# A planner that writes the instruction order of a fused attention and expert kernel: new prices, one shared port for VectorE and GpSimd, and a seeded first order

## The chip, the core and the metric

The kernel runs on one core of a Trainium2 chip. The core has five engines with one instruction queue each: TensorE (PE in the profile; PEld is its weight load), VectorE (DVE), ScalarE (ACT), GpSimd (POOL) and SyncE (SP), which here only issues transfers. Each engine takes its queue strictly in order and waits on semaphores where an instruction needs another engine's result. The metric is device time in microseconds (us), the median of several runs.

## The reference

Three parts follow each other. The intermediate values are float32, and every matrix product is made in float32 precision.

```python
q_n, k_n = (rmsnorm(q, g_q), rmsnorm(k, g_k))          # 4 batches, 12 heads, 448 tokens, 64 wide
scores = scale * np.matmul(q_n, k_n.transpose(0, 1, 3, 2))
attn = np.exp(scores - max) / sum
x = np.matmul(attn, v)                                  # laid out as 1792 tokens x 768
h = x @ w_in                                            # 768 x 2048
x = np.where(h > 0.0, h, np.exp(np.minimum(h, 0.0)) - 1.0) @ w_out
xn = x / rms * rms_g
out = (silu(xn @ w_gate) * (xn @ w_val)) @ w_out2       # 768 x 1536, twice, and back
```

## The kernel before

Attention is done in 24 **pairs** (two heads of one batch). A pair's steps are: load the tokens (`tk`), square them on ACT or POOL and sum the squares on DVE (`squares`), make the norm factors from the sums (`factors`, for several pairs at once, in `rr`), spread the factors along K (`spread`: for the first two pairs by small matmuls `bank<-ident,rr`, for all others by a round trip through DRAM, `scr<-rr` and `rb<-scr`), scale K (`rw<-rw,small,rb` on DVE), split Q and K into a high and a low part (`qh`, `ql`; pairs with odd numbers in the first batch use pieces of `gbig`), three matmuls per tile of scores (`s_group`), row maximum on DVE (`bank<-bank`, `nm`), exponential on ACT (`p`, `pj`, in odd pairs pieces of `tbig`), transposes on PE (`bank<-ident,p`), their copies out of PSUM (`pt`, `pe`), the product with V (`pv`), a multiplication with the reciprocal sums (`xf`) and a split into `xs`.

The expert layers are products `bank<-xs,w` and `bank<-gbig,w` with three matmuls each (high times high, high times low, low times high). They run in five stages: the first expert layers for batch 0, then for batch 1, the second ones for batches 0 and 1, and both again for batches 2 and 3, these last two stages with a scheme of seven products in place of eight (`quad`, with sums made ahead in `combos`). Weights are stored as 64-bit values. The first use of a chunk makes it into float32 (`w_convert`: two conversions on ACT or POOL, a mask and a merge on DVE: `wc`, `wt`) and keeps it in DRAM (`kept`); every use splits it into a high part (a copy on any engine, `w<-wc`) and a low part (a subtraction on DVE or POOL, `w<-wc,w`).

The order of all instructions on all engines is set by the class `Plan`. Each operation is entered with `plan.add`: the engines it may run on, a price in us for each, what it writes and reads. `schedule` then makes a first rank (the order of entry), plays the program through by `forward` (the engine that is free first takes the ready operation of the lowest rank; an operation that fits several engines goes to the one that would end it first), turns the result into new ranks by `backward`, and repeats this `PASSES` times. The play that ends first gives the order. The prices are written as functions: `c_v1` and `c_v2` for DVE, `c_a` for ACT, and numbers in place for POOL. Between dependent operations on different engines `LAT` is added. Two neighbours on DVE and POOL that both touch only SBUF stretch each other by the shares in `STRETCH`.

Of the kernel before, what the change touches and what calls it, by code (L numbers as in the profile page):

```python
# [35 lines left out]
class Plan:  # L36
# [4 lines left out]
    PASSES = 8  # L41
    LAT = 0.2
# [6 lines left out]
    STRETCH = {"v": 0.6, "g": 0.25}  # L49
# [36 lines left out]
    def add(self, alts, outs, ins, lag=0.0, after=None, soon=False, dma=False):  # L86
# [24 lines left out]
        shared = not any(getattr(ap.tensor, "_space", None) == PSUM for ap in list(outs) + list(ins) if ap is not None)  # L111
        self.ops.append((alts, preds, lag, soon, dma, shared))

    def schedule(self):
# [5 lines left out]
        best, rank = None, list(range(n))  # L120
# [10 lines left out]
    def backward(self, span, start, eng, price, lat):  # L131
# [8 lines left out]
        def avail(i):  # L140
            e, is_dma = eng[i], self.ops[i][4]
            r = 0.0 if self.succ[i] else lat[i]
            for s in self.succ[i]:
                if is_dma:
                    gap = lat[i] + 0.1
                elif eng[s] == e:
                    gap = 0.06 if e != "pe" else 0.0
                else:
                    gap = lat[i] + self.LAT
                r = max(r, left[s] + gap)  # L150
# [19 lines left out]
    def forward(self, rank):  # L170
# [14 lines left out]
        port = {"v": 0.0, "g": 0.0}  # L185
# [3 lines left out]
        def avail(i):  # L189
            for e in self.ops[i][0]:  # L190
                r = 0.0
                for j in self.ops[i][1]:
                    if self.ops[j][4]:
                        f = done[j] + 0.1
                    elif eng[j] == e:
                        f = done[j] - self.ops[j][2] + (0.06 if e != "pe" else 0.0)
                    else:
                        f = done[j] + self.LAT
# [7 lines left out]
        while left:  # L206
# [23 lines left out]
            i = heapq.heappop(now[e])[1]  # L230
            alts = self.ops[i][0]
            back[e] -= alts[e][0]
            if taken[i]:
                continue
# [11 lines left out]
            if e in self.STRETCH and self.ops[i][5]:  # L246

                o = "g" if e == "v" else "v"
                price += self.STRETCH[e] * max(0.0, min(port[o], t + price) - t)
                port[e] = t + price  # L250
# [11 lines left out]
            else:  # L262
                done[i] = free[e] + self.ops[i][2]
# [31 lines left out]
def kernel(ctx: ExitStack, tc: tile.TileContext, dims, tok, qk, vr, gq, gk, wst, rmsg, ident_in, out):  # L295
# [72 lines left out]
    def c_v1(n):  # L368
        return 0.15 + 0.00104 * n

    def c_v2(n):
        return 0.15 + 0.00052 * n

    def c_a(n):
        return 0.18 + 0.00083 * n

    def mm(o, l, r, start, stop, price=None):
        n = size(r)
        plan.add(
            {"pe": (price or max(0.108, n / 2400.0 + 0.017), lambda: T.matmul(o, l, r, start=start, stop=stop))},  # L380
            [o], [l, r] + ([] if start else [o]), lag=0.17,
        )

    def block(mms, price):
# [12 lines left out]
        plan.add({"pe": (price, go)}, list(outs.values()), list(ins.values()), lag=0.17)  # L397

    def transposes(pairs):
# [4 lines left out]
        plan.add({"pe": (0.02 + 0.11 * len(pairs), go)}, [o for o, _ in pairs], [i for _, i in pairs] + [ident], lag=0.17)  # L404

    def copy(dst, src, eng="vag"):
# [6 lines left out]
        if "a" in eng:  # L413
            alts["a"] = (c_a(n), lambda: A.activation(out=dst, in_=src, func=AF.Copy))
        if "g" in eng and not ps:
            alts["g"] = (
                0.2 + 0.00097 * n,
# [7 lines left out]
    def c_tt(a, b, n):  # L425
        return 0.2 + 0.0014 * n if two_sbuf(a, b) else c_v1(n)

    def tt(dst, a, b, op, eng="vg"):
# [4 lines left out]
        if "g" in eng and two_sbuf(a, b):  # L433
            alts["g"] = (0.25 + 0.0022 * n, lambda: G.tensor_tensor(out=dst, in0=a, in1=b, op=op))
# [18 lines left out]
    def act(dst, src, func, extra=0.0, accum=None, after=None, **kw):  # L453
        if accum is not None:
            kw["accum_out"] = accum
        plan.add(
            {"a": (c_a(size(src)) + extra, lambda: A.activation(out=dst, in_=src, func=func, **kw))},
# [3 lines left out]
    def vop(price, fn, outs, ins, after=None):  # L461
        plan.add({"v": (price, fn)}, outs, ins, after=after)

    def recip(dst, src):
        vop(0.15 + 0.00625 * size(dst), lambda: V.reciprocal(dst, src), [dst], [src])
# [164 lines left out]
    def w_convert(n):  # L630
# [13 lines left out]
                "a": (c_a(WN), lambda: A.activation(out=c, in_=Hf, func=AF.Copy, scale=2.0**-112)),  # L644
                "g": (
                    0.2 + 0.00097 * WN,
# [7 lines left out]
                "a": (0.3 + 0.001 * WN, lambda: A.activation(out=tl, in_=l8, func=AF.Copy, scale=1.0 / 32, bias=-15.5 / 32)),  # L654
                "g": (
                    0.3 + 0.00105 * WN,
# [780 lines left out]
```

## Time and profile before

| what | value |
|---|---|
| median of 3 runs | 1271.13 us (1270.31 to 1271.68) |
| the profiled execution, its own time | 1273.35 us |
| its span, first to last instruction | 1271.6 us |
| PE busy | 1231.3 us, 97% of the span, 6300 matmuls |
| POOL busy | 919.1 us, 72% |
| DVE busy | 835.1 us, 66% |
| ACT busy | 681.7 us, 54% |
| mean granted clock of TensorE | 0.993 |

PE is the engine that works nearly all the time; idle time of the other engines costs nothing as long as PE has work. Matmul ends are modelled, so a busy PE may hold short pauses. DVE and POOL are busy also while an instruction of theirs is held up after it was issued: two rows of one form with different durations show this.

### The profile page before, as it was taken

What the parts mean: (1) busy time and instruction counts of PE and PEld (TensorE: products, weight loads), DVE (VectorE), ACT (ScalarE), POOL (GpSimd) and SP (SyncE); (2) the same over time, 40 slices, a digit from 0 to 9 for tenths busy, and PEclk for the clock granted to TensorE, in tenths of its full rate; (3) what the DMA queues carried; (4) which work ended last, traced back from release to release, by engine and by line L of the source; (5) the groups of instructions that cost most, each with busy time, mean ns of one, the idle gap of its engine ahead of it and who ended that gap; (6) DMA issues with size and microseconds to landing.
All of it is one profiled execution on the core that took longest, in us unless ns stands there. A gap on an engine that the chain in (4) does not pass through costs nothing.

```text
span 1271.6 us, 17832 instructions
## 1 busy us (share of the span) xinstructions
PE 1231.3 (97%) x6300; PEld 1025.9 (81%) x6300; DVE 835.1 (66%) x1276; ACT 681.7 (54%) x1328; POOL 919.1 (72%) x688
## 2 busy tenths in 40 slices
PE   4998999999999999999999999999999999999998
PEld 2556867777777877898988888999999978999997
DVE  6886888879545588764554547626354899486582
ACT  5876767676655577554554543535334754342240
POOL 3587879997766697775653569948476999798680
PEclk9998999999999999999999999999999999999999
DMA  5677676775443444664444435212121112122112
GB/s 201 190 227 260 245 247 234 240 248 156 165 131 120 124 178 160 218 202 161 156 165 128 149 94 169 88 38 75 47 66 63 38 32 73 58 63 75 38 50 87
DMA packets 62206, 173.44 MB, mean 136 GB/s; under 512 B 10654, under 2 KB 19876, under 8 KB 62116
## 3 DMA queue, kind: packets, MB, share of 16 engines
q1 hardware_dynamic: 53476, 163.31, 39.3%
q10 hardware_dynamic: 8640, 8.99, 2.5%
q8 instruction: 49, 0.80, 0.2%
q14 instruction: 41, 0.34, 0.1%
HBM read 137.11 MB, written 35.17 MB: 135 GB/s over the span
## 4 chain that ended last, share of the span: by engine, by line
PE 79%; POOL 9%; DVE 4%; DMA 3%; issue 2%; ACT 1%; SPq 0%; ACTq 0%; POOLq 0%; DVEq 0%
PE bank L319 79%; POOL w L319 2%; POOL tbig L319 1%; POOL gbig L319 1%; POOL late L319 1%; POOL wr L319 1%; POOL xs L319 1%; DVE bank L319 1%; DMA rb<-scr 1%; DVE ybig L319 1%; POOL ql L319 1%; DMA tk<-tok 0%; DMA ybig<-tok 0%; DMA wc<-kept 0%; DMA wr<-wst 0%
## 5 line engine op out<-in xcount | busy, mean ns | idle before, releaser
L319 PE MATMUL bank<-xs,w 128*128 128x448 f32 x1872 | 423.0, 371 | 1.7 <-DVE tbig L319 0.9
L319 PE MATMUL bank<-gbig,w 128*128 128x448 f32 x1872 | 408.0, 372 | 2.8 <-POOL gbig L319 2.7
L319 PEld LDWEIGHTS bank<-gbig,w 128*128 128x128 f32 x1872 | 347.8, 189 | 43.0 <-issue 7.1
L319 PEld LDWEIGHTS bank<-xs,w 128*128 128x128 f32 x1872 | 344.6, 188 | 38.2 <-issue 6.7
L319 POOL TENSOR_TENSOR w<-wc,w 128x768 fp32r<-128x768 f32 (+1 forms) x126 | 241.8, 1921 | 81.1 <-ACT w L319 75.1
L319 DVE TENSOR_REDUCE bank<-bank 128x1 f32<-128x448 f32 x168 | 99.3, 624 | 76.2 <-PE bank L319 75.8
L319 ACT ACTIVATE w<-wc 128x768 fp32r<-128x768 f32 (+1 forms) x82 | 65.2, 795 | 91.7 <-PE bank L319 85.8
L319 DVE SCALAR_TENSOR_TENSOR wc<-wc,wt 128x768 int32<-128x768 int32 x68 | 92.2, 1356 | 26.9 <-ACT wc L319 16.5
L319 POOL TENSOR_TENSOR gbig<-tbig,gbig 128x448 fp32r<-128x448 f32 x75 | 99.8, 1333 | 8.7 <-ACT gbig L319 7.4
L319 ACT ACTIVATE p<-bank,nm,rr 128x448 f32<-128x448 f32 x126 | 90.2, 720 | 27.2 <-DVE nm L319 20.6
L319 POOL TENSOR_SCALAR w<-wc 128x768 fp32r<-128x768 f32 x65 | 60.9, 938 | 57.5 <-PE bank L319 51.6
L319 ACT ACTIVATE pt<-bank 128x384 f32<-128x384 f32 (+1 forms) x161 | 68.7, 448 | 50.6 <-PE bank L319 47.8
L319 DVE TENSOR_TENSOR tbig<-bank,tbig 128x448 f32<-128x448 f32 x80 | 48.5, 617 | 57.5 <-PE bank L319 55.4
L319 POOL TENSOR_TENSOR tbig<-tbig 128x448 f32<-128x448 f32 x45 | 59.5, 1324 | 28.3 <-DVE tbig L319 27.1
L319 DVE TENSOR_TENSOR ybig<-bank,ybig 128x448 f32<-128x448 f32 x72 | 44.4, 619 | 49.0 <-PE bank L319 48.8
L319 PE MATMUL bank<-ident,p 128*128 128x128 f32 x441 | 70.6, 277 | 5.4 <-ACT p L319 3.7
L319 PEld LDWEIGHTS bank<-ident,p 128*128 128x128 f32 x441 | 53.8, 141 | 23.0 <-ACT p L319 4.3
L319 PE MATMUL bank<-xs,late 128*128 128x448 f32 x288 | 69.5, 370 | 0.4 <-DVE xs L319 0.4
L319 DVE TENSOR_SCALAR wt<-wr 128x768 uint16<-128x768 uint16 x68 | 67.7, 995 | 1.5 <-DMA wr<-wst 1.2
L319 DVE SCALAR_TENSOR_TENSOR ybig<-bank,ybig 128x448 f32<-128x448 f32 x48 | 29.8, 622 | 55.1 <-PE bank L319 55.1
L319 PE MATMUL bank<-late,w 128*128 128x448 f32 x252 | 64.6, 368 | 0.0
L319 ACT ACTIVATE wt<-wr 128x768 uint16<-128x768 uint8 x42 | 45.7, 1089 | 28.6 <-DVE wc L319 20.7
(232 smaller groups left out, 2105.1 us busy)
## 6 DMA issues: line engine op xcount, KB each, us to landing
wr<-wst SPq DMA_DIRECT2D x68, 768.0 KB
wc<-kept SPq DMA_DIRECT2D x100, 384.0 KB
kept<-wc SPq DMA_DIRECT2D x68, 384.0 KB
rw<-qk SPq DMA_DIRECT2D x21, 512.0 KB
tk<-tok SPq DMA_DIRECT2D x20, 480.0 KB
rv<-vr SPq DMA_DIRECT2D x24, 256.0 KB
out_t<-ybig SPq DMA_DIRECT2D x24, 224.0 KB
rb<-scr ACTq DMA_DIRECT2D x36, 128.0 KB
```

The costliest lines, as they stand in the source:

```text
L319: return lambda *a, **k: f(*[real(x) for x in a], **{n: real(x) for n, x in k.items()})
```

## The change

All of it is in the planner and in the prices. No operation of the kernel is added or removed; which engine takes an operation, and in which place, may change. The change

- replaces `LAT` (0.2 for every hand-over between engines) by `HOP` (0.04 to 0.12, by receiving engine) and a `TAIL` that is added to the end of an operation but does not keep its engine;
- lets DVE and POOL share one `port`: every POOL operation takes it, and every DVE operation without PSUM operand unless it is marked `port=False` (reductions, reciprocals). While it is taken the other's operation waits and then is shortened by `BEHIND`. `STRETCH` goes;
- lets DVE take another ready operation, one that doesn't use the port, when the port is taken;
- prices an operation by the time from its issue to the next (`c_v1`, `c_v2`, `c_a`, new `c_gt` and `c_gs` for POOL), so nearly all prices fall;
- starts from the order of entry with seeded noise of up to 40 places, and makes 36 passes in place of 8.

```diff
-    PASSES = 8
-    LAT = 0.2
+    PASSES = 36
+    SEED = 20
+    HOP = {"pe": 0.12, "v": 0.04, "a": 0.04, "g": 0.09, "sp": 0.04}
+    TAIL = {"pe": 0.0, "v": 0.085, "a": 0.11, "g": 0.04, "sp": 0.0}
+    BEHIND = {"v": 0.15, "g": 0.05}
+    SLACK = 0.1
-    STRETCH = {"v": 0.6, "g": 0.25}
...
-        best, rank = None, list(range(n))
+        noise = random.Random(self.SEED)
+        best, rank = None, [i + 40 * noise.random() for i in range(n)]
...
+            if e == "v" and self.ops[i][5] and port > t + 0.1:
+                x = min((x for x in now["v"] if not taken[x[1]] and not self.ops[x[1]][5] and t + self.ops[x[1]][0]["v"][0] <= port + self.SLACK), default=None)
+                if x is not None:
+                    now["v"].remove(x)
+                    heapq.heapify(now["v"])
+                    heapq.heappush(now["v"], (rank[i], i))
+                    i = x[1]
...
-            if e in self.STRETCH and self.ops[i][5]:
-
-                o = "g" if e == "v" else "v"
-                price += self.STRETCH[e] * max(0.0, min(port[o], t + price) - t)
-                port[e] = t + price
+            if e == "g" or e == "v" and self.ops[i][5]:
+                if port > t:
+                    price = port - t + max(0.03, price - self.BEHIND[e])
+                port = t + price + self.TAIL[e]
...
-        return 0.15 + 0.00104 * n
+        return 0.064 + 0.00105 * n
...
-    def c_a(n):
-        return 0.18 + 0.00083 * n
+    def c_a(n, ps=False):
+        return (0.06 if ps else 0.1) + 0.00083 * n
+
+    def c_gt(n):
+        return 0.14 + 0.00216 * n
+
+    def c_gs(n):
+        return 0.155 + 0.00084 * n
...
-        return 0.2 + 0.0014 * n if two_sbuf(a, b) else c_v1(n)
+        return c_v1(n)
```

How many instructions each engine issues by the two orders: POOL 688 before and 607 now, ACT (its transfers included) 1279 and 1362, DVE 1276 and 1274, SP 388 and 388. What moved most: 36 copies of 128x768, 18 of 128x448 and 5 squarings of 128x960 from POOL to ACT, 16 additions or subtractions of 128x448 and 4 of 128x512 from POOL to DVE, 18 small copies out of PSUM from DVE to ACT.

Three places show what that does. The first is on POOL, where the first expert layer begins and pair 6 is prepared: `ql<-rw,qh` makes the low part of pair 6's K, `w` and `wc` are weights, `gbig<-tbig` are pieces of the hidden layer. Before:

```order
L319 TENSOR_TENSOR xs_75<-xf_124,xs_74 128x448
L319 TENSOR_SCALAR w_96<-wc_93 128x768
L319 TENSOR_SCALAR wc_92<-wr 128x768
L319 TENSOR_TENSOR w_96<-wc_93,w_96 128x768
L319 TENSOR_SCALAR w_97<-wc_94 128x768
L319 TENSOR_SCALAR wc_93<-wr 128x768
L319 TENSOR_TENSOR ql<-rw_101,qh 128x512
L319 TENSOR_SCALAR wt_95<-wr 128x768
L319 TENSOR_TENSOR gbig<-tbig,gbig 128x448
```

and now:

```order
L331 TENSOR_SCALAR wt_95<-wr 128x768
L331 TENSOR_SCALAR w_96<-wc_93 128x768
L331 TENSOR_TENSOR w_96<-wc_93,w_96 128x768
L331 TENSOR_TENSOR gbig<-tbig,gbig 128x448
L331 TENSOR_SCALAR gbig<-tbig 128x448
L331 TENSOR_SCALAR qh<-rw_101 128x512
L331 TENSOR_TENSOR gbig<-tbig,gbig 128x448
L331 TENSOR_TENSOR ql<-rw_101,qh 128x512
L331 TENSOR_TENSOR gbig<-tbig,gbig 128x448 x2
```

The weight work that stood between pair 6's high part and its low part is gone from there; one subtraction of 128x448 stands between them, and three `gbig` instructions are ahead of `ql`.

The second place is PE in the first pairs. `ident,rr` with 64x128 is the spread of the factors of pair 1, `qh` is pair 0, `gbig` is pair 1, `ident,p` are the transposes of pair 0. Before:

```order
L319 MATMUL bank7_132<-ident_61,rr0_112 64x128 x8
L319 MATMUL bank6_131<-ident_61,pj0_107 128x128 x3
L319 MATMUL bank6_131<-ident_61,pj0_107 64x128
L319 MATMUL bank1_126<-qh_103 128x448
L319 MATMUL bank2_127<-qh_103 128x448
...
L319 MATMUL bank4_129<-ident_61,p0_105 128x128 x3
L319 MATMUL bank6_131<-ident_61,p0_105 128x128 x3
L319 MATMUL bank3_128<-gbig_88 128x448 x3
L319 MATMUL bank5_130<-ident_61,rs0_119 7x128
```

and now (the spread of pair 1 stands above, right behind that of pair 0 and ahead of all matmuls of scores):

```order
L331 MATMUL bank6_131<-ident_61,pj0_107 128x128 x3
L331 MATMUL bank6_131<-ident_61,pj0_107 64x128
L331 MATMUL bank1_126<-qh_103 128x448
L331 MATMUL bank2_127<-qh_103 128x448
...
L331 MATMUL bank3_128<-gbig_88 128x448 x3
L331 MATMUL bank6_131<-ident_61,p0_105 128x128 x3
L331 MATMUL bank4_129<-ident_61,p0_105 128x128 x3
L331 MATMUL bank0_125<-gbig_88 128x448
```

The spread of pair 1 left its place between the scores, and three matmuls of pair 1 now stand ahead of pair 0's transposes.

The third place is ACT's queue where the factors of pairs 6 to 11 go to DRAM (`scr<-rr`; `tk` is a squaring of the tokens of a later pair). Before:

```order
L319 ACTIVATE ybig<-bank_131 128x384
L319 ACTIVATE tk_100<-tk_100 128x960
L319 ACTIVATE w_99<-wc_92 128x768
L319 DMA scr_148<-rr_113 128x8
L319 DMA scr_152<-rr_113 128x8
```

and now:

```order
L331 ACTIVATE wt_95<-wr 128x768
L331 ACTIVATE w_99<-wc_92 128x768
L331 ACTIVATE tk_100<-tk_100 128x960
L331 DMA scr_148<-rr_113 128x8
L331 ACTIVATE wt_95<-wr 128x768
L331 ACTIVATE xs_74<-xf_124 128x448
L331 DMA scr_152<-rr_113 128x8
```

In both a squaring that needs a transfer stands just ahead of the first `scr<-rr`. Counted from the start, 127 instructions of ACT are ahead of it before and 148 now, and squarings of batch 2's tokens are two before and three now.

## Rows read from the trace of the kernel before

**Rows 1.** The page's first part: busy time, share of the span, instructions.
```profile
PE 1231.3 (97%) x6300; PEld 1025.9 (81%) x6300; DVE 835.1 (66%) x1276; ACT 681.7 (54%) x1328; POOL 919.1 (72%) x688
```
**Rows 2.** Stretches: length, busy PE, PEld, DVE, ACT, POOL (instructions), PE's clock, DMA.
```profile
0.00:20.00 20.00, 4.92 (x25) 3.42 (x27) 11.96 (x34) 8.56 (x9) 5.08 (x9) 1.00 0.68 248
20.00:100.00 80.00, 72.60 (x422) 39.73 (x420) 67.15 (x159) 62.66 (x161) 51.86 (x47) 0.98 0.62 199
100.00:140.00 40.00, 35.40 (x160) 28.69 (x158) 27.09 (x33) 24.64 (x44) 30.90 (x22) 0.91 0.79 264
170.00:180.00 10.00, 7.80 (x33) 5.90 (x33) 7.75 (x11) 6.87 (x15) 9.84 (x8) 0.83 0.70 241
260.00:320.00 60.00, 56.66 (x292) 43.72 (x291) 52.36 (x85) 39.90 (x79) 50.99 (x37) 1.00 0.62 196
320.00:1000.00 680.00, 679.42 (x3503) 580.10 (x3502) 381.34 (x586) 351.99 (x679) 460.71 (x351) 1.00 0.39 126
1000.00:1090.00 90.00, 86.98 (x410) 76.72 (x409) 88.71 (x93) 50.28 (x86) 89.49 (x60) 0.98 0.16 49
1090.00:1272.00 182.00, 178.03 (x867) 162.34 (x865) 103.99 (x142) 54.51 (x86) 123.77 (x89) 1.00 0.19 61
```
**Rows 3.** Timeline at 11 us, DVE and POOL: start, duration, instruction.
```profile
11.79 1.14 DVE L319 SCALAR_TENSOR_TENSOR sn<-sn,rr 128x15 f32<-128x15 f32 x1
...
11.63 1.27 POOL L319 TENSOR_TENSOR gbig<-wr,gbig 128x512 fp32r<-128x512 f32 x1 [2.53 <-ACT gbig L319]
```
**Rows 4.** Timeline of PE, 20 to 31 us; in brackets idle time before, and releaser.
```profile
22.65 1.97 PE L319 MATMUL bank<-ident,rr 128*64 128x128 f32 x16
...
28.18 0.33 PE L319 MATMUL bank<-ident,p 128*128 128x128 f32 x1 [0.84 <-ACT p L319]
29.95 0.76 PE L319 MATMUL bank<-ident,p 128*128 128x128 f32 x4 [1.44 <-ACT p L319]
```
**Rows 5.** Timeline of PE, 112 to 122 us.
```profile
118.75 0.47 PE L319 MATMUL bank<-ql,qh 128*128 128x448 f32 x1 [2.89 <-POOL ql L319]
...
121.41 1.11 PE L319 MATMUL bank<-gbig,w 128*128 128x448 f32 x2 [0.70 <-POOL gbig L319]
```
**Rows 6.** Timeline of POOL, the same stretch.
```profile
114.36 1.55 POOL L319 TENSOR_SCALAR w<-wc 128x768 fp32r<-128x768 f32 x1
115.87 0.89 POOL L319 TENSOR_SCALAR wc<-wr 128x768 f32<-128x768 f32 x1
116.72 1.98 POOL L319 TENSOR_TENSOR ql<-rw,qh 128x512 fp32r<-128x512 f32 x1
```
**Rows 7.** Two stretches of 10 us, columns as in rows 2.
```profile
120.00:130.00 10.00, 9.30 (x36) 6.61 (x35) 9.12 (x13) 7.45 (x16) 9.92 (x7) 0.70 0.76 235
...
1020.00:1030.00 10.00, 7.84 (x29) 5.59 (x28) 10.00 (x7) 5.70 (x12) 10.00 (x7) 0.85 0.00 1
```
**Rows 8.** Timeline, 1013 to 1025 us: POOL, DVE, PE.
```profile
1013.89 1.54 POOL L319 TENSOR_TENSOR late<-ybig,late 128x448 fp32r<-128x448 f32 x1
1015.38 1.54 POOL L319 TENSOR_TENSOR tbig<-tbig,rsb 128x448 f32<-128x448 f32 x1
...
1014.33 1.57 DVE L319 TENSOR_TENSOR ybig<-ybig 128x448 f32<-128x448 f32 x1
...
1024.41 0.68 PE L319 MATMUL bank<-late,late 128*128 128x448 f32 x2 [0.94 <-POOL late L319]
```
**Rows 9.** Groups by form: count, busy us, mean ns, idle before and releasers.
```profile
L319 POOL TENSOR_SCALAR w<-wc 128x768 fp32r<-128x768 f32 x65 | 60.9, 938 | 57.5 <-PE bank L319 51.6 <-DVE wc L319 2.7 <-DVE nm L319 1.5
...
L319 ACT ACTIVATE w<-wc 128x768 fp32r<-128x768 f32 x70 | 59.0, 843 | 81.9 <-PE bank L319 76.0 <-issue 3.1 <-DMA wc<-kept 2.1
```
**Rows 10.** Who waited for whom: total us, times, longest.
```profile
PEld bank L319 <- ACT p L319: 6.5, 7, 1.6
```
**Rows 11.** The chain that ended last, 91 to 101 us: start, length, what.
```profile
91.50 5.91 DMA tk<-tok
...
97.50 3.72 DMA scr<-rr
```

More of the change, by code (lines that the diff above doesn't have):

```diff
@@ L84, in region, with add @@
         return ap.name, halves, m
-    def add(self, alts, outs, ins, lag=0.0, after=None, soon=False, dma=False):
+    def add(self, alts, outs, ins, lag=0.0, after=None, soon=False, dma=False, port=True):
         i = len(self.ops)
@@ L110, in add @@
                 self.hist[name] = keep
-        shared = not any(getattr(ap.tensor, "_space", None) == PSUM for ap in list(outs) + list(ins) if ap is not None)
+        shared = port and not any(getattr(ap.tensor, "_space", None) == PSUM for ap in list(outs) + list(ins) if ap is not None)
         self.ops.append((alts, preds, lag, soon, dma, shared))
@@ L184, in forward @@
         taken = [False] * n
-        port = {"v": 0.0, "g": 0.0}
+        port = 0.0
         dma_free = 0.0
@@ L194, in avail @@
                         f = done[j] + 0.1
-                    elif eng[j] == e:
-                        f = done[j] - self.ops[j][2] + (0.06 if e != "pe" else 0.0)
+                    elif e == "pe" and eng[j] == "pe":
+                        f = done[j] - self.ops[j][2]
                     else:
-                        f = done[j] + self.LAT
+                        f = done[j] + self.HOP[e]
                     r = max(r, f)
@@ L262, in forward @@
             else:
-                done[i] = free[e] + self.ops[i][2]
+                done[i] = free[e] + self.ops[i][2] + self.TAIL[e]
             dur[i], lat[i] = price, done[i] - t - price
@@ L379, in mm @@
         plan.add(
-            {"pe": (price or max(0.108, n / 2400.0 + 0.017), lambda: T.matmul(o, l, r, start=start, stop=stop))},
-            [o], [l, r] + ([] if start else [o]), lag=0.17,
+            {"pe": (price or max(0.108, n / 2400.0 + 0.0165), lambda: T.matmul(o, l, r, start=start, stop=stop))},
+            [o], [l, r] + ([] if start else [o]), lag=0.16,
         )
@@ L396, in block @@
             ins[id(l)], ins[id(r)] = l, r
-        plan.add({"pe": (price, go)}, list(outs.values()), list(ins.values()), lag=0.17)
+        plan.add({"pe": (price, go)}, list(outs.values()), list(ins.values()), lag=0.16)
     def transposes(pairs):
@@ L402, in go @@
                 T.transpose(o, i, ident)
-        plan.add({"pe": (0.02 + 0.11 * len(pairs), go)}, [o for o, _ in pairs], [i for _, i in pairs] + [ident], lag=0.17)
+        plan.add({"pe": (0.02 + 0.11 * len(pairs), go)}, [o for o, _ in pairs], [i for _, i in pairs] + [ident], lag=0.16)
     def copy(dst, src, eng="vag"):
@@ L455, in act, with vop @@
             kw["accum_out"] = accum
+            extra += 0.09
+        if any(hasattr(kw.get(k), "tensor") for k in ("scale", "bias")):
+            extra += 0.09
         plan.add(
-            {"a": (c_a(size(src)) + extra, lambda: A.activation(out=dst, in_=src, func=func, **kw))},
+            {"a": (c_a(size(src), in_psum(src)) + extra, lambda: A.activation(out=dst, in_=src, func=func, **kw))},
             [dst, accum], [src] + [x for x in kw.values() if hasattr(x, "tensor") and x is not accum], after=after,
         )
-    def vop(price, fn, outs, ins, after=None):
-        plan.add({"v": (price, fn)}, outs, ins, after=after)
+    def vop(price, fn, outs, ins, after=None, port=False):
+        plan.add({"v": (price, fn)}, outs, ins, after=after, port=port)
     def recip(dst, src):
-        vop(0.15 + 0.00625 * size(dst), lambda: V.reciprocal(dst, src), [dst], [src])
+        vop(0.1 + 0.00625 * size(dst), lambda: V.reciprocal(dst, src), [dst], [src])
     def dma(dst, src, nbytes, after=None, soon=False, by="sp"):
@@ L661, in w_convert @@
         )
-        vop(0.15 + 0.00104 * WN, lambda: V.tensor_scalar(out=th, in0=h16, scalar1=0x8000, scalar2=None, op0=ALU.bitwise_and), [th], [h16])
+        vop(c_v2(WN), lambda: V.tensor_scalar(out=th, in0=h16, scalar1=0x8000, scalar2=None, op0=ALU.bitwise_and), [th], [h16], port=True)
         stt(ci, ci, 3, ti, ALU.logical_shift_left, ALU.bitwise_or)
```

38 lines of the change are left out of this document (20 added, 18 removed).

## Prediction

> **What bounds the kernel now.** I read the page's busy times first, then a table by stretches, then the timeline of PE where that table shows it idle. PE is busy for 1231.3 of 1271.6 us [rows 1], so 40.3 us is all the idle time that a better order could win, and no other engine is near that share. Where it lies is in [rows 2], length less PE's busy time: 15.1 us before 20 us (first loads and first norm), 7.4 between 20 and 100 (attention of batch 0 alone), 4.6 from 100 to 140 (the expert layer starts), 2.2 at 170 to 180, 3.3 from 260 to 320, 0.6 in the 680 us to 1000, 3.0 from 1000 to 1090, and 3.6 at the end (the last result on its way out). What lies between these stretches is the missing 0.5. The first loads and the end don't depend on how the rest is ordered, save for a little at 10 to 20 us. So some 21 us is open. To it comes TensorE's clock. Behind idle time it was granted 1.2 in place of 2.4 GHz for short times: 0.70 on the mean of 120 to 130 us, behind the waits that ended at 118.75, and 0.85 at 1020 to 1030 [rows 5, 7]. By the clock column of [rows 2] this loses 0.02 x 80 + 0.09 x 40 + 0.17 x 10 + 0.02 x 90 = 8.7 us. Together 30 us, 2.4% of the span, is about the most that can be won, and two thirds of it lies in the first 320 us.
>
> Page and row differ on that ceiling. The Trainium skill ("Perfetto Trace Analysis", Identifying the Most-Contended Engine) calls matmul busy time a bad measure and weight-load busy time a good one: PEld has 81% of the span against 89% (162.34 of 182) in the last stretch, which would leave room for some 120 us, and a time near 1150 (1025.9 / 0.89). I don't follow it: from 20 to 100 us PEld is at 50% while PE is at 91% [rows 2], because transposes and products with V load weights for less time than they stream; the mix explains the difference. Short pauses inside busy time may exist all the same (a rival below).
>
> **The old plan's error.** A tiny DVE instruction of 15 elements took 1.14 us while POOL ran a subtraction from 11.63 to 12.90 [rows 3]: DVE was held until POOL was done. The old plan charges such a pair a share of the overlap; the new one charges the whole. Where the pieces of DVE and POOL alternate, one addition on each takes 1.49 us (POOL's starts at 1013.89 and 1015.38, the DVE addition between them 1.57) [rows 8]. So the new description of the port is the one the trace shows, and the new order should meet fewer surprises on those two engines. POOL also has less to do: 36 copies at 0.938 us are 33.8 us [rows 9], moved to ACT at 0.843.
>
> **The sum, stretch by stretch** (idle time plus clock is what can be won; the other bound in brackets):
>
> *0 to 20 us.* The spread of pair 1 costs PE 1.97 us at 22.65 [rows 4]. Now it stands ahead of the scores, while PE waits for K of pair 0 anyway. Against it, that order also makes the scores wait for what DVE does for pair 1, and a reduction stands ahead of the scaling of K. I take -1 (from -2 to +1).
>
> *20 to 100 us.* 7.4 idle and 1.6 clock. The two largest waits I see there, 0.84 and 1.44 us, are transposes that wait for the exponential [rows 4]; three matmuls of pair 1 now stand ahead of them and fill about 0.6 us. But ACT gets fuller: 21 more instructions ahead of the first `scr<-rr`, at 0.84 at most 17.6 us, on top of 62.66 busy of 80 [rows 2, 9]. That would be 80 of 80, by this high price. I take -2.5 (from -6 to +5; +5 if ACT becomes the bound and a third of the 17.3 us that it idled there stays on top of its 80, since it must go on waiting for DVE and PE at some points).
>
> *100 to 140 us.* 4.6 idle and 3.6 clock. PE waited 2.89 us for pair 6's `ql`, which stood on POOL behind a weight copy of 1.55 and a conversion of 0.89 and itself took 1.98 [rows 5, 6]. In the new order one `gbig` subtraction stands between `qh` and `ql`. 2.4 us of foreign work go, one piece of some 1.1 to 1.5 comes; and by the order of PE, 84 in place of 69 matmuls of the expert layer precede pair 6's scores, 15 more matmuls of cover. The wait should vanish, and with it the low clock behind it. K itself may still come late (its factors go out behind a squaring that waits for its tokens, as before: the load was under way for 5.91 us [rows 11]). I take -5 (from -8 to 0).
>
> *170 to 180 us.* 2.2 idle, 1.7 clock; the same kind of wait for POOL, which is busy 9.84 of 10 [rows 2]. I take -2.5 (from -3.9 to 0).
>
> *260 to 320 us.* 3.3 idle, clock full, POOL and DVE both at 51 to 52 of 60. POOL's copies moved to ACT, which has 20 us free there [rows 2]. I take -2 (from -3.3 to 0).
>
> *1000 to 1090 us.* 3.0 idle, 1.8 clock. DVE and POOL are at 98 and 99% [rows 2], so the port is the limit and PE waits for what it makes (0.94 us for `late` at 1024.41 [rows 8]). Here the two orders have nearly the same work: between the first and the last addition that reads `ybig`, 24 POOL and 20 DVE additions of 128x448 before, 25 and 18 now. The 12 of the 16 moved additions that lie in the last two stages are splits of `gbig`, elsewhere. So only the order inside can help. I take -1.5 (from -4.8 to +2).
>
> *New waits.* A new order meets its own surprises, where the old one had none: 140 to 170, 180 to 260, 320 to 1000 us. The prices of transfers are not changed by the diff, so their errors stay. I take +1.5 (0 to +6).
>
> Sum: -1 - 2.5 - 5 - 2.5 - 2 - 1.5 + 1.5 = **-13 us**: a span of 1258.6, a time of 1260.3 for an execution like the profiled one (its 1273.35 is 1.75 above its span). The median shown is 2.2 below that execution, so I forecast **1258 us**.
>
> **Rivals.**
>
> *More comes back* (1247). PE's busy time may hide pauses of a few tenths, since ends are modelled, and the first 320 us could give all of their idle and clock. For it: from 20 to 100 us the engines all have gaps at the same time, which points at the order and not at work. All 21 + 8.7 less the 6 of port-bound loss would be -24. Against it: ACT's load.
>
> *The waits only move* (1268). PE is at 97%, and each wait that goes may show the next one: K of pair 6 came by a chain of transfers (5.91 for tokens, 3.72 for the factors [rows 11]) whose prices stay as wrong as they were. Then 100 to 140 and 1000 to 1090 us gain nothing, the rest half: about -4, and with new waits -3.
>
> *Slower: ACT as the new bottleneck of attention* (1280). The change moves copies onto the engine that also does the exponentials and empties PSUM for PE. In the trace a wait of PE's weight load for `p` is 6.5 / 7 = 0.93 us [rows 10]; a copy of 0.843 us put in front of an exponential is of that size. One more such wait in each of 24 pairs is 22.3 us, and 22.3 - 13 = +9. It decides from 14 pairs on (14 x 0.93 = 13). Against it: after 320 us ACT is busy 352 of 680 us, and PE has expert matmuls beside the pairs to fill a late one; only 6 pairs stand alone.
>
> *The plan's description does no good* (within 0.2%, which is about what a measurement of this kernel can tell from no change). The list rule with 8 passes may already have found waits that only transfers cause. Against it: the rows at 118.75 and 1024.41 name POOL.
>
> **Chances and range.** Forecast, a gain of 6 to 19 us: 0.48. More: 0.14. Waits only move: 0.16, a quarter of it within 0.2% (2.5 us). No good: 0.06. Slower: 0.16, of which 0.02 is within 0.2%. That makes faster 0.74, same 0.12, slower 0.14. The range holds 8 in 10: below it a little of "more" (all 30 us would be 1241), above it the worse half of "slower". 1244 to 1273; the forecast's own range is 1252 to 1265.
>
> **What would show it.** Right: PE idle from 100 to 140 us under 2 us and its clock there above 0.97; `ql` of pair 6 on POOL within 2 us of its `qh`, with no wait of PE for it; tiny DVE instructions with means near their least; POOL's busy time down by some 50 to 90 us, ACT's up by some 45 to 70 (83 instructions more, at most at the 0.84 of a copy); the loss from 1000 to 1090 us nearly as before. Wrong: waits of PE or PEld for ACT `p` and `pt` above 15 us in total; ACT above 90% from 20 to 100 us with that stretch no shorter; a wait for `rb<-scr` ahead of pair 6 that holds PE for more than 3 us; new idle time of PE between 320 and 1000 us above 3 us.

## The result, and the profile after

The changed kernel takes 1261.41 us (median of 4 runs, 1256.58 to 1262.78) against 1270.72 us of the kernel before beside it: a ratio of 0.9919 (95% interval 0.9891 to 0.9947), 9.3 us faster. The forecast was 1258 us, in a range of 1244 to 1273. The profiled execution took 1256.58 us, the fastest of the four, with a span of 1254.8 us, 16.8 below that of before; so its rows show more than the typical gain (see the first experiment).

The page's first part, which answers to [rows 1]:

```profile
PE 1222.4 (97%) x6300; PEld 1026.5 (82%) x6300; DVE 832.4 (66%) x1274; ACT 729.1 (58%) x1411; POOL 837.2 (67%) x607
```

The stretches of [rows 2], with the same columns, in the changed kernel:

```profile
0.00:20.00 20.00, 2.63 (x20) 2.18 (x22) 11.78 (x35) 9.19 (x10) 4.09 (x8) 1.00 0.71 254
20.00:100.00 80.00, 77.61 (x429) 43.43 (x430) 62.07 (x152) 71.54 (x181) 40.60 (x37) 1.00 0.62 201
100.00:140.00 40.00, 35.89 (x169) 30.85 (x168) 26.30 (x36) 28.04 (x49) 22.91 (x18) 0.91 0.78 256
...
170.00:180.00 10.00, 9.80 (x61) 8.12 (x60) 8.90 (x16) 8.24 (x19) 9.45 (x7) 1.00 0.70 232
...
260.00:320.00 60.00, 58.79 (x316) 46.92 (x316) 47.96 (x81) 43.77 (x92) 48.21 (x37) 1.00 0.59 185
320.00:1000.00 680.00, 680.00 (x3511) 584.83 (x3510) 387.66 (x586) 386.19 (x728) 423.06 (x305) 1.00 0.39 124
1000.00:1090.00 90.00, 88.03 (x425) 78.93 (x425) 79.61 (x87) 45.02 (x74) 85.94 (x57) 1.00 0.20 60
```

POOL lost 82 us and ACT took 47, as forecast. PE's idle time went from 40.3 to 32.4 us, 7.9 less. The head got worse (idle 15.1 to 17.4), 100 to 140 us stayed (4.6 to 4.1, clock 0.91 both times), 20 to 100 got better by 5.0.

The clock column seems to give 5.1 us more (0.007 x 1271.6 = 8.9 us lost before, 0.003 x 1254.8 = 3.8 now), but it can't be used for the start. The trace's clock records begin at 26.95 us before and at 38.8 us now, and the column counts the time ahead of the first record as full clock. The pace of the matmuls tells otherwise. Timeline of PE, changed kernel, the same form at 35 and at 57 us:

```profile
35.41 1.49 PE L331 MATMUL bank<-gbig 64*128 64x448 f32 x6
...
57.08 0.86 PE L331 MATMUL bank<-gbig 64*128 64x448 f32 x6
```

Until 38 us PE ran at the pace of the lower level (1.2 GHz), and 1.49 in place of 0.86 us means that some 42% of such time is lost. With the time ahead of the first record counted, PE was busy at the lower level for 27.8 us before and 25.9 us now, which is an estimated loss of 11.7 and 10.9 us. So the clock gave about 1 us on the whole: some 2 us more lost before 100 us (15.3 and 20.6 us busy at the lower level), some 3 us less behind. PE's busy time fell by 8.9 us; 8.1 of them the clock doesn't explain, and what they were (pauses hidden by the modelled ends, perhaps) stays open.

Idle time alone misleads here, so here is the same table in long stretches, to be read by the matmuls that each holds (the number behind PE's busy time; 320 to 1000 us stands in [rows 2] and above). Before:

```profile
0.00:100.00 100.00, 77.52 (x443) 43.15 (x445) 79.10 (x192) 71.22 (x170) 56.93 (x56) 0.98 0.64 208
100.00:320.00 220.00, 209.39 (x1085) 163.60 (x1082) 181.91 (x268) 153.71 (x308) 188.18 (x135) 0.98 0.71 233
...
1000.00:1320.00 320.00, 265.00 (x1275) 239.06 (x1273) 192.70 (x234) 104.78 (x172) 213.26 (x148) 0.99 0.15 49
```

and after:

```profile
0.00:100.00 100.00, 80.24 (x447) 45.60 (x448) 73.85 (x187) 80.73 (x191) 44.69 (x44) 1.00 0.64 212
100.00:320.00 220.00, 212.92 (x1130) 168.53 (x1129) 181.27 (x275) 169.38 (x345) 170.22 (x124) 0.98 0.72 239
...
1000.00:1320.00 320.00, 249.21 (x1217) 227.56 (x1216) 189.63 (x229) 92.78 (x148) 199.23 (x136) 1.00 0.15 49
```

By 100 us only 4 matmuls more were done (0.8 us): what the idle time gained there, the clock took back. From 100 to 320 us there are 45 more, at 220 / 1130 us each 8.8 us. From 320 to 1000 it is 8 more, 1.6 us. Behind 1000 us one matmul takes 254.8 / 1217 = 0.2094 in place of 271.6 / 1275 = 0.2130 us, 4.4 us over 1217. That is 15.6 of the 16.8 us; a short matmul counts like a long one, so each part is good to some 2 us.

**The head.** PE before, first spread of factors and first scores:

```profile
13.84 1.98 PE L319 MATMUL bank<-ident,rr 128*64 128x128 f32 x16 [7.99 <-DVE rr L319]
17.37 0.74 PE L319 MATMUL bank<-qh 128*128 128x448 f32 x1 [1.56 <-POOL qh L319]
```

and now, DVE and PE, 9 to 22 us (columns as in [rows 3]):

```profile
9.35 0.17 DVE L331 SCALAR_TENSOR_TENSOR sn<-sn,rr 128x15 f32<-128x15 f32 x1
10.99 1.15 DVE L331 TENSOR_REDUCE ss<-ybig 128x15 f32<-128x960 f32 x1 [1.47 <-ACT ybig L331]
12.06 1.15 DVE L331 SCALAR_TENSOR_TENSOR rr<-sn,rr 128x15 f32<-128x15 f32 x1
...
15.58 1.98 PE L331 MATMUL bank<-ident,rr 128*64 128x128 f32 x16 [10.02 <-DVE rr L331]
...
19.89 1.98 PE L331 MATMUL bank<-ident,rr 128*64 128x128 f32 x16 [2.34 <-DVE rr L331]
21.80 0.74 PE L331 MATMUL bank<-qh 128*128 128x448 f32 x1
```

The factors of pair 0 stood still from 9.52 to 12.06 us, because the sum of another pair's squares (`ss<-ybig`) was put ahead of their next step and its tokens had not come. The first spread is 1.7 us later than before. The larger part of the 4.4 us by which the scores are late lies behind it: the spread of pair 1 now stands ahead of them, and PE waited 2.34 us for its factors and worked on it for 1.98, while pair 0's `qh` was ready at 19.02.

**Pair 6.** Timeline, 104 to 119 us, of SP, ACT, POOL, DVE and PE:

```profile
104.68 0.33 SPq L331 DMA_DIRECT2D tk<-tok  x1
...
109.63 1.01 ACT L331 ACTIVATE tk<-tk 128x960 f32<-128x960 f32 x1 [1.07 <-DMA tk<-tok]
...
113.97 0.62 POOL L331 TENSOR_SCALAR qh<-rw 128x512 fp32r<-128x512 f32 x1 [0.67 <-DVE rw L331]
114.30 0.91 ACT L331 ACTIVATE wc<-wr 128x768 f32<-128x768 f32 x1 [2.31 <-POOL gbig L331]
114.32 0.73 DVE L331 TENSOR_SCALAR wt<-wr 128x768 uint16<-128x768 uint16 x1 [0.43 <-DMA wr<-wst]
114.56 1.47 POOL L331 TENSOR_TENSOR gbig<-tbig,gbig 128x448 fp32r<-128x448 f32 x1
115.99 1.26 POOL L331 TENSOR_TENSOR ql<-rw,qh 128x512 fp32r<-128x512 f32 x1
117.31 0.96 DVE L331 TENSOR_TENSOR w<-wc,w 128x768 fp32r<-128x768 f32 x1 [2.26 <-ACT w L331]
118.86 3.35 PE L331 MATMUL bank<-gbig,w 128*128 128x448 f32 x8 [4.09 <-DVE tbig L331]
```

`ql` no longer holds PE: it starts 2.0 us behind its `qh`, and nothing waits for it. But PE waits 4.09 us a few instructions earlier (its weight load 4.46), for a piece of the hidden layer. The chain that ended last passes here:

```profile
98.55 6.06 DMA scr<-rr
...
104.68 4.87 DMA tk<-tok
```

A load of tokens was issued only when the factors that ACT had sent had landed (the program lets both count on the same semaphore, and SyncE's queue stood at it until 104.63). ACT stood 1.07 us for those tokens, then 2.31 us ahead of a weight, with PE's work behind it in its queue. The row at 114.30 names POOL, whose last piece was done at 113.31; DVE's reading of the same weight, at 114.32, waits for the transfer. The factors took 6.06 us, in place of 3.72 [rows 11].

**The port.** Timeline of POOL and DVE, 1018 to 1022 us:

```profile
1019.40 2.23 POOL L331 TENSOR_TENSOR w<-wc,w 128x768 fp32r<-128x768 f32 x1
...
1019.84 0.61 DVE L331 TENSOR_TENSOR rsb<-bank,tbig 128x448 f32<-128x448 f32 x1
1020.37 0.61 DVE L331 TENSOR_TENSOR tbig<-bank,tbig 128x448 f32<-128x448 f32 x1
1020.90 1.14 DVE L331 TENSOR_TENSOR wr<-wc,wr 128x384 f32<-128x384 f32 x1
```

Under one POOL subtraction DVE does two additions with an operand in PSUM (`bank`) at 0.61 us each; the shorter one with both operands in SBUF ends only behind POOL's end at 1021.63. The Trainium skill ("SBUF — State Buffer", Who interferes with whom) states that a DVE instruction with two SBUF inputs contends with a GpSimd one that reads SBUF, and that one with at most one SBUF input, outside its two-port modes, does not; these rows agree. The holding itself did not get rarer for tiny instructions. The group `rs<-sm` (24 of them, least 0.150 us), first before, then after:

```profile
L319 DVE TENSOR_SCALAR rs<-sm 128x7 f32<-128x7 f32 x24 | 15.6, 651 | 7.3 <-ACT p L319 7.2
```

```profile
L331 DVE TENSOR_SCALAR rs<-sm 128x7 f32<-128x7 f32 x24 | 15.4, 642 | 10.7 <-ACT p L331 10.6
```

It did get rarer for one large form: the 68 merges of weights (`wc<-wc,wt`, two operands in SBUF) take 1188 in place of 1356 ns on the mean, 11.4 us of DVE in all.

### The profile page after: what moved, and what is told of

Its sections match the earlier page's. It is cut to its first block, busy times and chain, and to the rows that moved or that the text cites. A ratio compares the mean times of both kernels' runs of the same rounds, so it can differ in the third digit from the quotient of the medians.

```text
span 1254.8 us, 17810 instructions
## 1 busy us (share of the span) xinstructions
PE 1222.4 (97%) x6300; PEld 1026.5 (82%) x6300; DVE 832.4 (66%) x1274; ACT 729.1 (58%) x1411; POOL 837.2 (67%) x607
## 4 chain that ended last, share of the span: by engine, by line
PE 86%; POOL 4%; DMA 3%; DVE 3%; ACT 3%; issue 1%; SPq 0%; ACTq 0%; POOLq 0%; DVEq 0%
PE bank L331 86%; DMA wr<-wst 1%; POOL w L331 1%; DMA kept<-wc 1%; ACT p L331 1%; POOL gbig L331 1%; DMA ybig<-tok 1%; ACT ybig L331 0%; POOL tbig L331 0%; DMA scr<-rr 0%; DVE bank L331 0%; DVE ss L331 0%; DMA tk<-tok 0%; DVE rw L331 0%; DVE wc L331 0%
## 5 line engine op out<-in xcount | busy, mean ns | idle before, releaser
L331 POOL TENSOR_TENSOR w<-wc,w 128x768 fp32r<-128x768 f32 (+1 forms) x124 | 233.9, 1887 | 120.0 <-ACT w L331 117.0
L331 ACT ACTIVATE w<-wc 128x768 fp32r<-128x768 f32 (+1 forms) x110 | 89.0, 809 | 98.3 <-PE bank L331 90.4
L331 DVE SCALAR_TENSOR_TENSOR wc<-wc,wt 128x768 int32<-128x768 int32 x68 | 80.8, 1188 | 44.0 <-ACT wc L331 40.0
L331 POOL TENSOR_TENSOR gbig<-tbig,gbig 128x448 fp32r<-128x448 f32 x68 | 90.7, 1336 | 18.3 <-ACT gbig L331 15.3
L331 ACT ACTIVATE pt<-bank 128x384 f32<-128x384 f32 (+1 forms) x167 | 71.4, 445 | 27.0 <-PE bank L331 26.3
L331 ACT ACTIVATE wt<-wr 128x768 uint16<-128x768 uint8 x48 | 52.3, 1090 | 26.4 <-DVE wc L331 19.6
L331 DVE TENSOR_SCALAR wt<-wr 128x768 uint16<-128x768 uint16 x68 | 64.9, 955 | 3.8 <-DMA wr<-wst 3.5
L331 POOL TENSOR_SCALAR w<-wc 128x768 fp32r<-128x768 f32 (+1 forms) x38 | 36.4, 959 | 36.8 <-PE bank L331 31.6
```

The lines of the kernel that those rows point to most:

```text
L331: return lambda *a, **k: f(*[real(x) for x in a], **{n: real(x) for n, x in k.items()})
```

## The experiments

The theory: the plan now charges what the port costs, and a longer search over a right description finds orders with fewer and shorter waits of PE. Rivals: seed 20 is a lucky draw; the longer search alone does it; the new prices do it without the port; transfers and ACT set what is left. Each ratio is to the kernel before, run beside it.

| kernel | what differs | ratio (95% interval) |
|---|---|---|
| again | changed kernel | 0.9924 (0.9905 to 0.9944) |
| nosearch | changed, 8 passes, no seed | 0.9991 (0.9978 to 1.0005) |
| noseed | changed, no seed | 0.9931 (0.9913 to 0.9949) |
| seed4 | changed, seed 4 | 0.9908 (0.9891 to 0.9925) |
| seed4p8 | changed, seed 4, 8 passes | 0.9946 (0.9928 to 0.9963) |
| searchonly | before, seed 20, 36 passes | 1.0017 (1.0008 to 1.0026) |
| noport | changed, old port rule | 1.0337 (1.0313 to 1.0360) |
| nopick | changed, DVE never out of turn | 1.0025 (1.0015 to 1.0036) |
| head | changed, pair 0's factors first | 0.9908 (0.9892 to 0.9923) |
| lanes | changed, transfers of both queues counted | 0.9947 (0.9932 to 0.9961) |
| sqpool | changed, squarings on POOL | 0.9967 (0.9955 to 0.9980) |
| headlanes | head and lanes, 60 passes | 0.9903 (0.9884 to 0.9923) |

**again.** 

> The changed kernel once more, unchanged. Its four runs gave 1256.6 to 1262.8 us at mean granted clocks of 0.997 to 0.990. Theory A (the clock makes the spread): time times clock is nearly constant, about 1250 to 1253 us; the runs lie at 1255 to 1264 and each 0.001 of clock goes with about 1 us; the profile, if its clock is near 0.99, shows the low clock behind a wait of PE that the first profile does not have. Theory B (transfers that land at other times): runs of equal clock differ by 3 us or more. Ratio expected 0.990 to 0.994 by both.

Six runs, 1257.81 to 1264.62 us, median 1260.63. The profiled one has a span of 1262.8 and a clock of 0.992. Two stretches of it, and the same two of the first profile:

```profile
30.00:40.00 10.00, 9.69 (x43) 5.71 (x42) 7.62 (x29) 9.53 (x24) 3.26 (x4) 0.60 0.20 62
50.00:60.00 10.00, 8.28 (x40) 4.67 (x38) 7.62 (x18) 8.12 (x22) 1.72 (x2) 0.75 0.67 215
```

```profile
30.00:40.00 10.00, 9.58 (x41) 6.17 (x40) 7.60 (x27) 9.53 (x24) 3.42 (x4) 1.00 0.17 54
50.00:60.00 10.00, 8.50 (x54) 4.90 (x54) 9.54 (x22) 9.93 (x28) 3.64 (x4) 1.00 0.76 224
```

From 50 to 60 us the difference is real: the lower level holds for part of the stretch in the second execution, and it has 40 matmuls in place of 54. From 30 to 40 us it is one of the records alone. They begin at 24.4 us in this profile and at 38.8 us in the first, and the matmuls are equally slow in both; PE here:

```profile
34.50 1.49 PE L331 MATMUL bank<-gbig 64*128 64x448 f32 x6
```

With the time ahead of the records counted, PE was busy at the lower level for 26.6 us here and 25.9 in the first profile. So theory A falls: the clock makes some 0.3 of the 8.0 us between the spans, and 5.1 are idle time of PE (1262.8 - 1225.3 = 37.5 against 32.4). The ten runs say the same: time times clock goes from 1248.8 to 1256.1 us, as wide as the times, and runs with a clock of 0.997 took 1256.58 and 1259.88. Theory B has its sign; which transfers landed later was not followed. In this second profile 432 matmuls were done by 100 us, 11 fewer than before the change; so the 0 to 100 us bring nothing that is sure.

**nosearch, noseed, seed4, seed4p8.** First order and passes:

```diff
-    PASSES = 36
+    PASSES = 8
-        best, rank = None, [i + 40 * noise.random() for i in range(n)]
+        best, rank = None, list(range(n))
```

(nosearch both; noseed the second alone; seed4 `SEED = 4`; seed4p8 that and the first.)

> New prices and port, but the first order is the order of entry and 8 passes, as before the change. Theory A (the prices and the port carry the gain): 1257 to 1266 us, that is 5 to 14 us below the kernel before. Theory B (the longer and seeded search carries it): within 3 us of the kernel before, 1268 to 1274.

> The changed kernel with the plain order of entry as first order, but 36 passes. Theory A (with the right description any long search gains): 1258 to 1264 us, as the changed kernel. Theory B (the seed is a lucky draw): 1266 to 1271 us, as the new prices with 8 passes gave (1269.0).

> The changed kernel with another seed (4 in place of 20), 36 passes. Theory A (the description and a long search gain): 1258 to 1264 us. Theory B (seed 20 is a lucky draw): between 1265 and 1271 us, with two to four new waits of 1 to 3.5 us each in other places, as nosearch has at 465 and 1028 us.

> Seed 4 with 8 passes in place of 36 (the new prices and port as they are). The new prices without seed gave no gain with 8 passes (0.9991) and the full one with 36 (0.9931). Theory A (few passes leave the order unfinished): 1266 to 1271 us. Theory B (an order with 8 passes is as good as one with 36, and the one run was an unlucky draw): 1257 to 1263 us, as seed 4 with 36 passes (1259.6).

With 36 passes all three first orders gave the gain: 1260.97 without a seed, 1259.61 with another. So seed 20 is no lucky draw. With 8 passes the new prices gave 1269.01 us, where theory B of nosearch had it, and 1262.64, where theory B of seed4p8 had it: a short search can find a good order or miss it. In these two pairs 36 passes are worth 0.9991 - 0.9931 = 0.6% and 0.9946 - 0.9908 = 0.4% of 1271 us, some 5 to 8 us; the two orders with 8 passes differ by as much. The order of nosearch has waits like this one of PE (timeline at 1027 us), which the changed kernel lacks:

```profile
1027.71 0.88 PE L331 MATMUL bank<-late,late 128*128 128x448 f32 x3 [3.27 <-POOL late L331]
```

**searchonly.** The second line of that diff and the passes, put into the kernel before. 

> The kernel before with 36 passes and the seeded first order, old prices and old shares of stretching. Theory A (prices and port): within 4 us of the kernel before, of either sign, with tiny DVE instructions still stretched and POOL still near 900 us busy. Theory B (search): 5 to 12 us faster.

1272.85 us, a little slower than before. The same search, with this seed, gains nothing with the old description. Theory B falls.

**noport.** The old rule in place of the new:

```diff
-            if e == "g" or e == "v" and self.ops[i][5]:
-                if port > t:
-                    price = port - t + max(0.03, price - self.BEHIND[e])
-                port = t + price + self.TAIL[e]
+            if e in self.STRETCH and self.ops[i][5]:
+                o = "g" if e == "v" else "v"
+                price += self.STRETCH[e] * max(0.0, min(port[o], t + price) - t)
+                port[e] = t + price
```

(and the out-of-turn rule taken out). 

> The changed kernel with the old description of the port (DVE and POOL stretch each other by a share of the overlap, and DVE takes nothing out of turn), all else as changed. With the low new prices this plan believes that DVE and POOL work side by side nearly freely. Theory A (the shared port matters): slower than the changed kernel by 5 us or more, the loss from 1000 to 1090 us (two fast stages) above 6 us of PE idle, POOL busier by some 30 us. Theory B (only the prices per instruction and the hand-over matter, the port does not): within 3 us of the changed kernel.

1314.57 us, 3.4% slower than before: more than the theory asked for. Idle time appears even in the stretch that had none:

```profile
320.00:1000.00 680.00, 667.39 (x3414) 565.55 (x3415) 366.87 (x558) 356.68 (x674) 408.66 (x302) 1.00 0.38 123
1000.00:1090.00 90.00, 82.79 (x388) 74.61 (x387) 78.72 (x88) 55.52 (x96) 84.14 (x62) 0.96 0.15 46
```

and where DVE and POOL alternate (timeline at 1046 us), ACT waits for a DVE addition that took 1.42 us, and PE 2.04 us for ACT:

```profile
1046.34 1.38 POOL L325 TENSOR_TENSOR wr<-wc,wc 128x384 f32<-128x384 f32 x1
1046.78 1.42 DVE L325 TENSOR_TENSOR ybig<-ybig 128x448 f32<-128x448 f32 x1
1048.23 0.58 ACT L325 ACTIVATE xs<-ybig 128x448 fp32r<-128x448 f32 x1 [2.40 <-DVE ybig L325]
1049.33 0.47 PE L325 MATMUL bank<-late,late 128*128 128x448 f32 x1 [2.04 <-ACT late L325]
```

The lower prices are what DVE and POOL take alone; without the port the plan believes in both at once. The port with the old prices was not tried, so how much of the gain the new prices make stays open.

**nopick.** The seven lines of the change that let DVE take another operation are taken out; the port stays. 

> The changed kernel without the rule that lets VectorE take an operation out of turn that doesn't use the port; the shared port itself stays. Theory A (what counts is that the plan charges the port): 1258 to 1265 us. Theory B (the gain is the out-of-turn rule, which fills VectorE while GpSimd holds the port): 1267 us or more, with more PE idle between 1000 and 1090 us (over 5 us).

1273.61 us: the whole gain is gone, as theory B had it, but not in the place that it named. From 1000 to 1090 us PE is idle for 2.9 us, not over 5. The loss is spread: 34 matmuls fewer than in the changed kernel by 320 us (454 and 1089 against 447 and 1130), 33 fewer from 320 to 1000,

```profile
320.00:1000.00 680.00, 676.68 (x3478) 576.89 (x3477) 383.91 (x582) 371.47 (x707) 421.52 (x304) 1.00 0.39 125
```

with single waits such as 3.19 us for `p` at 235.41. DVE is busy for 843.3 in place of 832.4 us, which explains nothing by itself: seed4p8 has 850.3 and a gain. It is one order; the six orders with the rule and 36 passes lie between 0.9908 and 0.9967, so a draw is an unlikely cause, but how much is the rule's own stays open.

**head.** The sums of squares of pairs 1 to 5 get one dependency more:

```diff
-        vop(c_v1(15 * D), lambda: V.reduce_sum(out=ss, in_=tk3, axis=AX.X), [ss], [tk])
+        vop(c_v1(15 * D), lambda: V.reduce_sum(out=ss, in_=tk3, axis=AX.X), [ss], [tk], after=first.get(i))
...
+        if b == 0 and k0 == 0:
+            first.update(dict.fromkeys(range(1, 6), len(plan.ops) - 1))
```

> The changed kernel with one dependency more: the sums of squares of pairs 1 to 5 come behind the norm factors of pair 0 on VectorE. In the changed kernel two of these sums stand ahead of the last steps of the factors, and one waits 1.47 us for a squaring whose tokens land at 9.93 us. Theory A (the head is a wrong guess of the landing of the first tokens): the first spread starts at 9 to 11 us in place of 15.6, the first scores at 13 to 18 in place of 21.8, and the time is 3 to 8 us below the changed kernel. Theory B (the 80 us behind are bound by ScalarE, 89% busy there, or by the other pairs' tokens): scores start earlier, but the time is within 2 us of the changed kernel, since PE waits longer between 20 and 100 us.

```profile
10.11 1.98 PE L331 MATMUL bank<-ident,rr 128*64 128x128 f32 x16 [3.07 <-DVE rr L331]
...
13.60 0.74 PE L331 MATMUL bank<-qh 128*128 128x448 f32 x1 [1.51 <-ACT qh L331]
```

The scores start at 13.60 in place of 21.80 us (timeline of PE), 8.2 us earlier; the time is 1259.59, 1 to 2 us below the changed kernel and inside its interval. The late head is no matter of one draw: in seven orders without this edit (nosearch, noseed, seed4, seed4p8, nopick, lanes, sqpool) the scores start between 19.9 and 21.6 us. In this order the spread of pair 1 also stands behind the first scores again (at 22.95 us), so both delays of the head go at once. PE is then idle for 6.95 us from 20 to 100 in place of 2.39, but by matmuls the lead is still there at 100 us: 471 against 447. It shrinks to 10 by 320 us (1116 against 1130 in that stretch) and is gone by 1000 (3498 against 3511). The cause of the late head is shown; what the mend wins is given back between 100 and 1000 us, and why stays open.

**lanes.** The limit of 8 counted over both queues:

```diff
-                if e == "sp":
-                    if len(flight) == self.FLIGHT:
-                        free[e] = max(free[e], flight.popleft())
+                if len(flight) == self.FLIGHT:
+                    free[e] = max(free[e], flight.popleft())
+                if e == "sp":
```

(and `flight.append` for both). 

> The changed kernel with the planner's limit of 8 transfers under way counted over the transfers of both queues (SyncE's and ScalarE's), in place of SyncE's alone. In the trace a load of tokens at 104.68 us was issued only when the factors that ScalarE had sent at 98.55 had landed (6.06 us), and ScalarE then stood 1.07 us for those tokens ahead of work for PE. Theory A (this coupling makes the wait of 4.46 us at 118.86): that wait falls under 2 us and the time is 2 to 6 us below the changed kernel. Theory B (what is wrong is the time of the transfers, 6 to 9 us here against the plan's 2 to 7): the wait stays at 3 us or more, the time within 3 us of the changed kernel.

```profile
100.00:140.00 40.00, 38.98 (x198) 33.23 (x195) 30.84 (x42) 28.87 (x52) 26.94 (x21) 1.00 0.85 285
...
1000.00:1090.00 90.00, 84.22 (x396) 74.53 (x395) 82.23 (x87) 42.04 (x71) 80.22 (x56) 0.98 0.17 53
```

The wait at pair 6 is gone (1.0 us idle from 100 to 140, clock 1.00, 198 matmuls in place of 169), as theory A had it; the time is 1264.33, as theory B had it. That the edit made the wait go is not shown: it is absent from six orders without the edit too (nosearch, noseed, seed4, seed4p8, nopick and sqpool have 1.3 to 2.3 us of idle time there and no wait above 1.4 us). The new order waits elsewhere: 5.8 us of idle from 1000 to 1090.

**sqpool.** `squares` of pairs 6 to 23 without ACT as a choice (`plan.ops[-1][0].pop("a")`). 

> The changed kernel with the squarings of the tokens of pairs 6 to 23 on GpSimd alone. From 40 to 80 us ScalarE is busy for 39.6 of 40 us in the changed kernel, 4 of them with four such squarings, and GpSimd for 22. Theory A (ScalarE is the limit of that stretch): ScalarE has 4 us less there and the stretch gets shorter by 1.5 us or more; the time is 1 to 4 us below the changed kernel. Theory B (ScalarE is full because it may be, PE waits for chains of several engines): no shorter; a squaring takes GpSimd about 2.2 us in place of 1.0 on ScalarE and holds the port, so the time is the same or up to 5 us more, with the waits for pair 6 larger.

```profile
40.00:60.00 20.00, 19.35 (x117) 10.26 (x116) 17.18 (x41) 18.84 (x53) 9.97 (x8) 1.00 0.53 162
60.00:80.00 20.00, 18.20 (x112) 10.04 (x110) 17.68 (x42) 19.70 (x54) 15.76 (x14) 1.00 0.78 285
```

1266.50 us, slower than the changed kernel. Squarings went, other copies came: ACT is still busy for 38.5 of 40 us, and PE for 37.55. The run speaks for theory B in the time, but since ACT stayed full it does not tell whether ACT is the limit there; that stays open.

**headlanes.** Both edits, and 60 passes in place of 36. 

> Both mends together: the sums of squares of pairs 1 to 5 behind pair 0's factors, and the limit of 8 transfers counted over both queues; 60 passes. Apart they gave about -1.5 us (scores 8 us earlier, most of it given back) and +3 us (the wait at pair 6 gone, others new) against the changed kernel. Theory A (each mends a wrong price and the rest is the luck of one draw): 1252 to 1258 us, scores at 13 to 14 us, PE idle from 100 to 140 us under 2 us. Theory B (PE's idle time is a sum of small waits that any order of this planner has): 1258 to 1264 us, with 28 us or more of PE idle in all.

1258.82 us (1253.19 to 1262.11). The smallest median of all, but not to be told from the changed kernel, seed4 or head by the intervals. The scores start at 15.67 us, not at 13 to 14, and PE is idle for 1.5 us from 100 to 140. In all it is idle for 1256.7 - 1220.8 = 35.9 us of the profiled span, as theory B had it.

## Why the prediction was right, and where not

**The sum came out, its parts less so.** It gave -13 us; the two profiles show -16.8 and -8.8, the medians -9.3.

- *0 to 20 us*: -1 forecast, +2.3 measured, 1.3 above the upper bound. The step took the spread that moved for a gain and the scores' wait for pair 1 for a smaller cost. It was the other way round: the spread ahead of the scores, with its wait of 2.34 us, made some 2.7 of the 4.4 us by which they are late. The sum ahead of pair 0's factors (a wait of 1.47 us for tokens and 1.15 for itself, in the queue of DVE) came on top.
- *20 to 100 us*: -2.5 forecast. Idle time went from 7.4 to 2.4 us in the first profile and to 4.2 in the second, but by matmuls 0 to 100 us gain nothing sure. The step counted 1.6 us of clock from a column that has no records ahead of 26.95 us. By 42% of PE's time at the lower level, 20 to 100 us lost an estimated 4.4 us before, and 7.5 and 8.6 in the two profiles: the loss grew.
- *100 to 140 us*: -5 forecast, -0.5 measured. The wait for `ql` went, as worked out (115.99 less 113.97 is 2.0 us behind `qh`). The rival *the waits only move* was right here: the chain of transfers made the next wait. Their prices, which the term for new waits left as they were, stayed wrong.
- *170 to 180 and 260 to 320 us*: -2.5 and -2 forecast, -3.7 and -2.1 measured. With what lies between, 100 to 320 us gave 8.8 us in the first profile and, by its 30 matmuls more, 5.9 in the second: most of the gain.
- *1000 to 1090 us*: -1.5 forecast; idle 3.0 to 2.0 and the clock to 1.00, -2.8. DVE, which the step took for full (88.71 of 90 us), is busy for 79.61 there, with 425 matmuls in place of 410: the order could win more than the step allowed.
- *New waits*: +1.5 forecast; 180 to 260 us +0.9, 320 to 1000 us -0.6. So this term was too high by about 1 us.

That the total came within 4 us is in part luck. The sum adds up idle time and clock. Of the 16.8 us in the first profile, idle time gave 7.9 and the clock some 0.8; of the 8.8 in the second, 2.8 and some 0.5. The other 8.1 and 5.5 us came out of PE's busy time, for which the sum has no term; only the rival *more comes back* named such pauses. They made up for the head and for 100 to 140 us, which gave 7.8 us less than forecast.

The ceiling of 30 us rests on the same clock column, which has no record for the first 26.95 us, with PE busy at the lower level for 11.9 of them. And of those 30 us, 24 and not 20 lay in the first 320 us, by the prediction's own terms.

**The reason given was half of it.** "The new order should meet fewer surprises" was to follow from the description of the port. With that description and 8 passes one order gained nothing that is sure (0.9991) and another 0.5% (0.9946). The full gain came with the description, the search (5 to 8 us) and, in the one order tried, the out-of-turn rule. And DVE's tiny instructions are held as long as before (642 against 651 ns): that sign was wrong. The port's cost is entered in the plan and only in part avoided (the merges of weights, 11.4 us); taking it out, together with the rule, costs 4% against the changed kernel (1.0337 / 0.9919), and taking out the rule alone 1%. Of the other signs, POOL's and ACT's busy times came out; PE's idle time (4.1 us) and clock (0.91) from 100 to 140 us did not.

**Slower through ACT** did not come. PE's own waits for `p` are 0.5 us from 20 to 100, PEld's 4.9 in the whole run, against 6.5 [rows 10], though ACT is 99% busy from 40 to 80 us; for `pt` PEld waits 6.7 us against 4.5, so the two together stayed the same. What held ACT's queue up for PE were transfers, of tokens (1.07 us) and of a weight (2.31 us). **More comes back** (1247) did not come either: no order here has less than 32 us of idle time of PE. The time near 1150 us was not come near either: no run took less than 1253.19 us, and PEld is busy for 82% as it was for 81%. The prediction estimated it from weight-load busy time, the measure that the Trainium skill ("Perfetto Trace Analysis", Identifying the Most-Contended Engine) prefers to matmul busy time. No run here set out to fill that room, so whether it is there stays open.

## What to carry to other kernels

A planner's price for a shared resource matters as a whole: lower prices without the port and the out-of-turn rule made the kernel 3.4% slower, and the search without any of them gained nothing. Once one wait is mended, read the same place again before its gain is booked: here the head was mended by 8.2 us and the time hardly moved. Before an edit is said to have removed a wait, look whether other orders without the edit have it. Compare two orders by work done up to a time as well as by idle time, and take a second profile: two executions of one order had spans 8.0 us apart. Where the clock is read from a column, check it by the pace of one form of matmul.

## What was not expected of the hardware

In both executions of the changed order PE ran at the pace of the lower clock level until about 38 us (in the second with a break of 3.4 us from 24.4 on), though it was busy for 9.58 and 9.69 of 10 us from 30 to 40; in the head run, whose scores start 8.2 us earlier, the clock is full from 21.3 us on, but for 3.4 us at 1014.6. From 50 to 60 us one execution kept the full clock and the other did not (1.00 and 0.75), with PE busy for 8.50 and 8.28 of 10 us. And a transfer of 4 KB of factors was under way for 6.06 us at 98.55 us, longer than the 480 KB of tokens behind it (4.87).
